# Sliding-window attention and a token mixer: q^T kept in even and odd tokens, the stores cut in four to undo it

## The chip, the cores and the metric

The kernel runs on one core of a Trainium2 chip. The metric is the device time of one execution in microseconds (us); runs of a kernel are compared by their median. One execution is also taken by the hardware profiler; its trace names TensorE (PE, with its weight loads as PEld), VectorE (DVE), ScalarE (ACT), GpSimd (POOL) and SyncE (SP), and the DMA queues that POOL and SP issue to.

## What is computed

Eight batches, eight heads, 576 tokens, head dimension 64. Attention looks back over a window of 128 tokens and subtracts a slope times the distance. Its output, 512 wide, is x for a token mixer: a weight for each pair of tokens from two small projections, the mix over all tokens, a ReLU, and an output projection.

```python
scores = scale * np.matmul(q, k.transpose(0, 1, 3, 2))
bias = slopes[:, None, None] * (-np.abs(rel).astype(np.float32))[None, :, :]
mask = (rel >= 0) & (rel < window)            # window = 128
attn = softmax(np.where(mask, scores + bias[None], -1e9))
x = np.matmul(attn, v)                        # (B, H, S, D) -> (B, S, H * D)
W_tok = scale * np.einsum('bsd,btd->bst', x @ w_q, x @ w_k)
out = np.maximum(np.einsum('bst,btd->bsd', W_tok, x), 0.0) @ w_out
```

The mixer's sum over t runs over all tokens, so the order in which tokens lie there does not matter to it; the rows of `out` come in the order of the rows s.

## The kernel before

All work is a list of 796 small operations, written down batch by batch (`load_qk`, `load_v`, `transposes`, `attention` with `values`, `mixing`). A string of numbers, `ORDER`, then fixes the order in which they are emitted, and so the order on each engine: `57P7` is operation 57 on TensorE with its result in PSUM bank 7, `62A` operation 62 on ScalarE, D is VectorE, G is POOL, S is SyncE; `+13/7` puts 13 matmuls on zeros ahead (`keep`), which fill a wait. Every engine works through its own list in order and waits on semaphores for what an operation needs. Nothing is moved while it runs.

The stages of a batch:

- Loads (L239), all issued by POOL, cast fp32 to f16 on the way. q and k of batches 1 to 5 come in pair form: a partition holds two neighbouring tokens, 128 elements in one run for each head. For batches in `ONE` (6 and 7) a partition holds one token, 64 elements a run, and there are twice as many issues of half the size. The last 64 tokens of q and k come in one tile `ntl`. Batch 0 has six tokens to a partition, in space borrowed from `osa`.
- Transposes (`tqk`, L366 in pair form and L360 in one-token form; `tqkt` L382 for the tail) put q^T and k^T in PSUM, even tokens ahead of odd ones where pairs were loaded. The copy out of PSUM (`etqk`, on ScalarE L220 or VectorE L222) puts them in token order into `qkT`: its source is read with a stride of 128 elements between neighbours.
- `sc` (L415): scores of two heads in eight or ten small matmuls, k^T as weights, a strip of q^T moving. Columns of a strip are queries. `exp` (L420) on ScalarE, `edge` (L435) and `mul` (L439) on VectorE multiply with `bt`, the exponentials of slope times distance, made from `rel` (an iota, L245).
- `pv` (L459) multiplies with v, whose extra column gives the softmax sum; `rec` and `nrm` (L472, L475) normalize into x; `xt` (L491) transposes x, `ext` copies it out.
- `mixing`: `wqk` (L508), `wkt` (L526), `g` (L538), `mx` (L554) with its ReLU `emx`, then `po` (L575): four matmuls for 128 rows of the output of a pair of batches. `eo` copies the bank into one of 14 tiles of `osa`, and `st` (L582) is its store, issued by SyncE. There are 36 of each; a tile is used again for the store 14 later, after the earlier one has landed.

SyncE has nothing but the stores. They stand in its queue in the order of `ORDER`, and at the head stands operation 318, which waits for copy 317 on ScalarE. SyncE's DMAs use eight semaphores in turn, so a store also waits for the one eight issues before it to land.

Of the kernel before, what the change touches and what calls it, by code (L numbers as in the profile page):

```python
# [13 lines left out]
P = 128  # L14
S = 576
# [11 lines left out]
0D 1D 32G 2G 28G 3D 22D 31G 4D 30G 29G 33G 137G 23D 6A 9A 53P7+13/7 35G 7A 11A 45P6 34G 134G 51P5+4/0 136G 52A  # L27
49P4 21G 50D 47P5+3/0 46D 133G 72P0 48A 74P2 55P4 132G 8A 5A 54A 40G 63P5+3/6 75A 59P7 39G 60D 12A 73A 36G 13D
61P2+3/2 16D 76D 43G 57P1+1/7 62A 56D 149P7 17G 64A 38G 147P0 85P2 58A 65D 135G 148D 18A 94P4 86A 150D 145P6
44G 95A 96P2+1/0 146D 83P0 97A 143P5+1/7 37G 10A 77D 42G 144A 14D 41G 78P2+1/4 84A 98D 228G 79D 186P6+3/4 80D  # L30
26G 87D 164P4+2/0 19D 99D 25G 151P3+1/0 165A 142G 66D 100P0 15A 152A 138G 88D 67P4 187A 188P2 139G 101D 68D
102D 189A 89P6 140G 69D 175P0 81P3 176A 141G 90D 166P4 91D 103P2 229G 104A 82D 92P7+2/0 190D 177P0 167A 153P2
232G 191D 178A 70P6+1/6 227G 24D 240P5+2/4 168D 71A 93D 231G 154A 179D 105P6+1/0 180D 321G 20A 241A 155P0 169D
230G 106A 107A 320G 108P5+1/2 170P2 109A 192P6 322G 156A 193D 244P5 194D 324G 110P4 181P0 171D 319G 172D 111A
245A 112P6 416G 182D 157D 114P2 238P4 115A 158D 242P5 323G 113A 118P2 239A 119D 159P6 234G 243D 195P3 160D
183D 270P4 246P2 235G 161D 116P0 247A 117D 173P7 336P6 419G 174D 271A 272P0 337D 184P2 273A 338P7 418G 196A
274D 248P0 250P4 237G 275D 332P6 249A 251A 339D 283P0 233G 162P3 281P4 163A 252D 333D 185A 236G 282A 334P7
197P2 27G 253D 284A 259P4 329G 335A 198D 330P6 260A 414G 285D 200P7 431P1 199A 201D 261P4 325G 331D 432A 202P7
417G 262A 203D 353P0 340P2 286D 415G 210P6 354A 351P4 211D 352A 326G 254P0 263D 341A 276P6 255D 327G 256D
364P4 362P2 264D 363A 287P0 365A 328G 277D 129P3 288D 278D 342P4 511G 289D 130A 375P6 257P2 343A 265P0 510G  # L40
126P3 344D 376A 258D 601G 429P5 345D 290P4 127A 208P6 291A 266D 433P3 507G 267D 209A 425P2 355D 279P4 434A
366D 268P7 509G 373P0 280D 430A 269D 204P3 426D 374A 516G 206P6 427P5 207A 292P0 605G 356D 428A 346P6 508G
205D 293A 123P5 347D 294A 506G 348D 295P4 448P2 377D 296A 705G 435P0 124D 449A 297P7 421G 436A 459P4 298D
357P2 367D 424G 460A 301P0 457P6 302A 358D 368P4 359D 458A 602G 446P0 369D 468P2 447A 370D 521P7 422G 349P6
469A 378D 305P0 470P4 423G 471A 212P3 461D 350D 306A 522D 437P4 420G 472D 299P6 303P0 438A 519P2 304D 213A
523P5 439D 706G 520A 517P4 462D 379P0 610G 518A 300D 120P3 606G 380D 524A 221P2 381D 697G 121D 371P7 222A
616P6 698G 450D 372A 382P5 617D 527P0 383A 609G 360P4 451D 538P2 361A 525P7 604G 440D 528A 384P4 514G 539A
526D 560P0 385A 607G 452P2 386D 387P7 215P6 561A 603G 453D 388A 562P4 454D 608G 216A 529P0 389P7 563A 473D
699G 716P6 530A 441P2 564D 512G 540P4 717D 551P0 390D 620P6 513G 442D 552A 224P7 621D 565D 541A 515G 463P0
225A 443D 391P4 700G 549P6 464D 392D 622P3 550A 702G 444P2 623D 618P5 445A 703G 397P6 465D 393P3 624P2 398A  # L50
619D 704G 395P0 394A 712P7 531D 396A 626P5 701G 625D 637P3 627A 474P0 532D 615G 307P2 638A 475D 713D 639P5
613G 308A 476D 714P4 640A 614G 533P2 715D 650P0 612G 542D 628P6 310P5 534D 629A 553D 543D 611G 466P4 651A
720P7 707G 535D 311A 218P6 709G 721A 630D 648P0 641D 544P2 631D 711G 649A 718P7 545D 219A 708G 566P0 546D 719A
455P5 567D 313P6 710G 467D 456A 568D 733P2 735P4 554D 632P0 736A 316P7 633D 314A 634D 555P4 734A 724P0 317A
556D 722P2 477P6 557D 725A 318S 217S 125S 399P7 131S 128S 220S 478D 723A 744P0 642D 661P4 659P2 745A 411P6
652D 737D 400A 726D 405P1 660A 653D 401S 547P7 662A 727D 643P2 412A 569P0 548D 406A 479P4 413S 226S 644D 570A
645D 536P7 480D 558P6 408P3 559D 481A 482P2 537D 755P0 409D 483A 746P4 757P6 756A 663D 410S 571P2 214S 315S
664D 747A 484P1 758A 572D 665P4 485D 573A 748D 574P7 646P6 666D 575A 488P0 667D 490P2 489A 576P7 486P4 491A
728P0 577D 487A 647D 492P2 582P6 729D 635P5 730D 583A 494P4 493A 759D 578P0 636D 584P6 580P2 760D 579A 497P5
581A 738D 654P0 585A 761P2 495A 655D 656D 739P6 498A 496S 223S 122S 309S 407S 500P4 749D 731P5 740D 668P1 762D  # L60
741D 732A 402P0 669D 750P6 763D 742P5 403A 657P1 751D 752D 586P3 404S 312S 658A 764P2 743A 753P7 765D 670P0
754D 587D 766P6 671D 589P5 672D 767A 673P3 769P2 590D 503P1 674D 592P5 501D 504A 770D 675P3 768A 505S 499S
502S 588S 591S 771P4 676A 593A 677P0 683P2 772D 595P7 678A 594S 684D 775P4 773P0 596D 679P2 598P6 776A 680D
597S 774A 681P4 779P2 599A 777P0 685P7 682D 778A 600S 780D 694P6 686A 784P5 687S 695D 691P4 696S 785D 790P7
786S 692D 793P6 693S 791D 688P5 792S 794D 787P4 795S 689A 781P7 690S 788D 789S 782A 783S
# [86 lines left out]
ONE = (6, 7)  # L152
# [6 lines left out]
def kernel(  # L159
# [20 lines left out]

    bt = pool.tile([P, H, 512], F16, name="bt")
# [5 lines left out]
    vn = [pool.tile([P, NT, H, VW], F16, name=f"vn{i}") for i in range(NV)]  # L187
    qkT = [pool.tile([P, 2, 4, S], F16, name=f"qkT{i}") for i in range(NQ)]
# [52 lines left out]
    def setup():  # L241
# [3 lines left out]
                lambda e: nc.gpsimd.iota(rel, pattern=[[1, 256]], base=0, channel_multiplier=-1),  # L245
                writes=["rel"])
        plan.op("idn", ("DVE",),
                lambda e: nc.vector.tensor_scalar(out=idn, in0=rel[:, 0:128], scalar1=0, scalar2=None,
# [44 lines left out]
    def load_qk(b):  # L293
# [35 lines left out]
    def transposes(b):  # L329
        T = qkT[b % NQ]  # L330
        if b == 0:
            for hp in range(4):
                for x in range(2):
# [8 lines left out]
                    def ev(e, hp=hp, x=x, g=g):  # L342
                        cp(e, T[:, x, hp, :].rearrange("t (p j) -> t p j", j=6),
# [6 lines left out]
        for z in range(2):  # L350
            for x in range(2):
                g = Ps(1)

                def tr(e, z=z, x=x, g=g):
                    o = ps16(g).rearrange("t (y j p) -> t y j p", y=4, j=2)
                    if b in ONE:
# [11 lines left out]
                def ev(e, z=z, x=x, g=g):  # L368
                    if b in ONE:
# [268 lines left out]
```

## Time and profile before

| what | value |
|---|---|
| median of 3 runs | 147.66 us (147.45 to 148.08) |
| the profiled execution: time, and span of the program in it | 148.28 us, 146.2 us |
| busy in the span: PE, DVE, ACT, POOL | 134.8, 122.2, 109.6, 86.1 us |
| first and last store issue | 101.3 and 143.0 us |

Busy time is the time in which an engine worked, and its share is an average over stages. Matmuls are pipelined, so a busy PE is not one at its peak. The chain that ended last is followed back from the last instruction to what released it; the stages are read with tables by windows of time. SPq is SyncE's sequencer issuing a DMA: the time given is the issue, not the transfer.

### The profile page before, as it was taken

The page shows a single profiled execution, that of the slowest core. Times are in us where ns is not written, and L with a number is a line of the kernel's source. Part 1 is how long each engine was busy: PE and PEld are TensorE (multiplying, and loading weights), DVE is VectorE, ACT ScalarE, POOL GpSimd, SP SyncE. Part 2 cuts the span into 40 slices and gives each one's busy share as a digit, 9 for nine tenths or more (in the row PEclk, how much of TensorE's full clock was granted, in tenths as well). Part 3 has the DMA queues.
Part 4 walks back from the last instruction along what each step waited for, and adds up shares of the span by engine and source line. Part 5 has one row for each costly group of instructions (what it writes and reads, how often), then busy time and mean ns, then how long its engine had stood idle before and what let it go on. Part 6 is the DMA issues. An engine that isn't in the chain of part 4 may idle for free.

```text
span 146.2 us, 5403 instructions
## 1 busy us (share of the span) xinstructions
PE 134.8 (92%) x2319; PEld 87.9 (60%) x2319; DVE 122.2 (84%) x229; ACT 109.6 (75%) x172; POOL 86.1 (59%) x114
## 2 busy tenths in 40 slices
PE   6979889999898889999999999999989999999990
PEld 2444547667675566767667676676667577653430
DVE  3634899977999998999999999998989898868750
ACT  3329969897699987999999889899959872557121
POOL 6999999999578976898899999910000000000000
PEclk9999999999999999999999999999999999999997
DMA  2999999999999999999999999990957018329684
GB/s 28 135 171 178 162 142 140 132 162 179 178 173 159 178 178 164 166 169 173 154 153 137 149 152 155 136 128 12 378 193 281 8 59 300 147 97 376 259 321 172
DMA packets 90855, 24.59 MB, mean 168 GB/s; under 512 B 84176, under 2 KB 86224, under 8 KB 90832
## 3 DMA queue, kind: packets, MB, share of 16 engines
q0 software_dynamic: 85648, 14.82, 130.2%
q1 hardware_dynamic: 5184, 9.44, 17.4%
q8 instruction: 18, 0.29, 0.7%
q14 instruction: 5, 0.04, 0.1%
HBM read 29.62 MB, written 9.44 MB: 267 GB/s over the span
## 4 chain that ended last, share of the span: by engine, by line
PE 45%; ACT 20%; DVE 14%; DMA 10%; issue 6%; POOL 2%; SPq 1%; ACTq 0%; DVEq 0%; POOLq 0%
PE psb L575 15%; ACT pt L420 9%; PE psb L459 7%; DMA out_dram<-osa 6%; PE psb L415 5%; DMA osa<-in_k_dram 4%; DVE x L475 4%; PE psb L491 3%; ACT qkT L220 3%; ACT rm L561 3%; PE psb L360 3%; PE psb L366 3%; ACT xT L220 2%; PE psb L554 2%; PE psb L508 2%
## 5 line engine op out<-in xcount | busy, mean ns | idle before, releaser
L420 ACT ACTIVATE pt<-psb 128x768 f16<-128x768 f32 x64 | 49.8, 819 | 6.2 <-PE psb L415 5.2
L239 POOL DMA_DIRECT2D vn<-in_v_dram x44 | 36.6, 887 | 3.6 <-DMA natq<-in_q_dram 2.4
L575 PE MATMUL psb<-wout,rm 128*128 128x512 f16 x144 | 35.2, 379 | 0.2
L439 DVE TENSOR_TENSOR pt<-pt,bt 128x1536 f16<-128x1536 f16 x32 | 29.9, 949 | 0.2
L475 DVE TENSOR_TENSOR x<-psb,inv 128x640 f16<-128x640 f32 x32 | 26.0, 820 | 0.7
L459 PE MATMUL psb<-vn,pt 128*128 128x65 f16 x576 | 22.4, 193 | 1.6 <-DVE pt L439 0.5
L222 DVE COPY qkT<-psb 128x1024 f16<-128x1024 f16 (+2 forms) x23 | 18.7, 822 | 5.6 <-PE psb L339 5.1
L459 PEld LDWEIGHTS <-pt 128*128 128x128 f16 x576 | 20.1, 97 | 5.0 <-issue 1.2
L220 ACT COPY osa<-psb 128x512 f32<-128x512 f32 x23 | 13.3, 590 | 12.3 <-PE psb L575 6.9
L220 ACT COPY qkT<-psb 128x1024 f16<-128x1024 f16 (+2 forms) x20 | 17.8, 912 | 4.2 <-PE psb L339 2.9
L415 PE MATMUL psb<-qkT 64*64 64x192 f16 (+2 forms) x640 | 20.1, 234 | 0.9 <-ACT qkT L220 0.4
L575 PEld LDWEIGHTS <-rm 128*128 128x128 f16 x144 | 12.7, 98 | 12.7 <-issue 1.1
L415 PEld LDWEIGHTS <-qkT 64*64 64x64 f16 x640 | 11.6, 106 | 9.7 <-issue 7.0
L239 POOL DMA_DIRECT2D natk<-in_k_dram x18 | 16.2, 938 | 1.7 <-DMA natk<-in_k_dram 1.2
L239 POOL DMA_DIRECT2D natq<-in_q_dram x18 | 16.8, 938 | 0.0
L592 PE MATMUL psb<-wz 128*128 128x512 f16 x43 | 13.8, 427 | 1.5 <-DVE wz L242 1.3
L491 PE MATMUL psb<-idn,x 128*128 128x128 f16 x160 | 13.6, 219 | 0.9 <-ACT osa L220 0.5
L435 DVE TENSOR_TENSOR pt<-pt,bt 128x512 f16<-128x512 f16 x32 | 12.9, 414 | 1.2 <-ACT pt L420 1.0
L561 ACT ACTIVATE rm<-psb 128x576 f16<-128x576 f32 x21 | 12.8, 653 | 1.5 <-PE psb L554 1.0
L491 PEld LDWEIGHTS <-x 128*128 128x128 f16 x160 | 10.0, 98 | 3.9 <-issue 1.1
L222 DVE COPY osa<-psb 128x512 f32<-128x512 f32 x13 | 9.0, 689 | 2.7 <-PE psb L575 2.3
L220 ACT COPY xT<-psb 128x576 f16<-128x576 f16 x15 | 9.4, 647 | 1.8 <-PE psb L491 1.8
(62 smaller groups left out, 162.2 us busy)
## 6 DMA issues: line engine op xcount, KB each, us to landing
out_dram<-osa SPq DMA_DIRECT2D x36, 256.0 KB, 2.9
vn<-in_v_dram POOLq DMA_DIRECT2D x28, 128.0 KB, 4.9
natq<-in_q_dram POOLq DMA_DIRECT2D x10, 256.0 KB, 6.8
natk<-in_k_dram POOLq DMA_DIRECT2D x10, 256.0 KB, 7.2
vn<-in_v_dram POOLq DMA_DIRECT2D x16, 64.0 KB, 4.8
natq<-in_q_dram POOLq DMA_DIRECT2D x8, 128.0 KB, 5.2
natk<-in_k_dram POOLq DMA_DIRECT2D x8, 128.0 KB, 5.1
osa<-in_q_dram POOLq DMA_DIRECT2D x4, 144.0 KB, 4.1
```

The lines of the kernel that those rows point to most:

```text
L220: nc.scalar.copy(o, i)
L222: nc.vector.tensor_copy(out=o, in_=i)
L239: plan.op(name, ("POOL",), lambda e: nc.gpsimd.dma_start(out=dst, in_=src), reads=reads, writes=writes)
L415: nc.tensor.matmul(ps32(g)[half : half + 64, o : o + w], T[r, 1, hp, k0 : k0 + 64], T[r, 0, hp, q0 : q0 + w], start=True, stop=True)
L420: nc.scalar.activation(out=blocks(pt)[:, :, 2 * u : 2 * u + 2, 0:192], in_=ps32(g).rearrange("t (a c) -> t a c", a=2)[:, :, 0:384].rearran ...
L439: nc.vector.tensor_tensor(out=o, in0=o, in1=bt[:, 2 * hp : 2 * hp + 2, 0:192].unsqueeze(2).broadcast_to([P, 2, 4, 192]), op=ALU.mult)
L459: nc.tensor.matmul(ps32(g)[:, o : o + D + 1], pt[:, a, c : c + 128], vv[:, kb, 2 * hp + a, 0 : D + 1], **flags)
L475: nc.vector.tensor_tensor(out=xb[:, :, 128 * hp : 128 * hp + 128].rearrange("t j (a d) -> t a j d", a=2), in0=px()[:, :, :, 0:D], in1=iv.u ...
L491: nc.tensor.transpose(ps16(g)[:, 128 * t : 128 * t + 128], xb[:, t, 128 * hp : 128 * hp + 128], idn)
L561: nc.scalar.activation(out=o, in_=s, func=AF.Relu, scale=WSCALE)
L575: nc.tensor.matmul(ps32(g), rm[p % NR][:, db, o : o + 128], wout[:, db, :], start=(db == 0), stop=(db == 3))
L592: nc.tensor.matmul(psb[:, b, :], wz[:, 0:P], wz[:, 0:DM], start=True, stop=True)
```

## The change

q^T is no longer put in token order when it leaves PSUM. It is kept as all even tokens and then all odd ones, so the copy reads its source densely. The score matmul takes its strip from there in pieces of 32: for each 64 tokens, 32 even ones and then 32 odd ones. From there on, every strip, the table `bt` (through `rel`), x, and the rows of the output have this order inside each block of 64 tokens. k^T and v stay in token order. The identity `idn` is put together again from the permuted `rel`.

The output has to be in token order. A store of 128 rows holds two blocks of 64, each of 32 even and 32 odd tokens, and becomes four DMAs of 32 rows, each to every second row of `out`.

q is loaded in pair form for all batches from 1 on, and k in pair form for 1 to 3 and one-token form for 4 to 7 (`ONE`). The tail copy becomes two copies, one for q and one for k. `ORDER` is new throughout: 36 matmuls on zeros instead of 43, other places for loads, and other engines for some copies. Of the 28 copies `etqk`, VectorE had 8 strided and 6 dense ones and has 1 and 13; ScalarE had 12 and 2 and has 5 and 9. ScalarE takes over three `eo`, two `emx` and three `ewqk` on balance.

On SyncE, the stores around the 17th (`osa` is the tile, `out_dram` the output; DMAHW are the eight slots of SyncE's own queue, DMASW those of POOL's, the others the engine that copied the bank). Before, the 15th to the 19th:

```order
L582 DMA out_dram<-osa 128x512 [waits DMAHW6_49]
L582 DMA out_dram<-osa 128x512 [waits DMAHW7_49,DMASW0_49]
L582 DMA out_dram<-osa 128x512 [waits DMAHW0_49]
L582 DMA out_dram<-osa 128x512 [waits DMAHW1_49,Activation_49]
L582 DMA out_dram<-osa 128x512 [waits DMAHW2_49,DMASW0_49]
```

After, the 16th (from its second piece on), the 17th and the head of the 18th:

```order
L603 DMA out_dram<-osa 32x512 [waits DMAHW5_49]
L603 DMA out_dram<-osa 32x512 [waits DMAHW6_49]
L603 DMA out_dram<-osa 32x512 [waits DMAHW7_49]
L603 DMA out_dram<-osa 32x512 [waits DMAHW0_49,Activation_49]
L603 DMA out_dram<-osa 32x512 [waits DMAHW1_49]
L603 DMA out_dram<-osa 32x512 [waits DMAHW2_49]
L603 DMA out_dram<-osa 32x512 [waits DMAHW3_49]
L603 DMA out_dram<-osa 32x512 [waits DMAHW4_49,Activation_49]
```

What was one row is four, each with a slot of its own; only the first piece waits for the bank. In the new table the 17th store is 595 and its bank is copied by 594A; behind 594A stand 14 `po`, 8 `mx`, one `g` and one `wkt` on TensorE. Behind 317A, which the first store waits for in both, stand 7 `sc`, 7 `pv`, 13 `xt`, 23 `po`, 4 `wqk`, 4 `wkt`, 4 `g` and 16 `mx` before, and one `sc`, two `pv` and one `xt` more after.

On VectorE, around the copies of batch 0 (`qkT_82`) and batch 1 (`qkT_83`). Before:

```order
L222 COPY qkT_82<-psb 128x576
L435 TENSOR_TENSOR pt_86<-pt_86,bt 128x2x4x64
L222 COPY qkT_83<-psb 128x8x64
L222 COPY qkT_83<-psb 128x4x256 x2
L439 TENSOR_TENSOR pt_87<-pt_87,bt 128x2x4x192
L268 COPY bt<-bt 128x4x64 x2
```

After:

```order
L224 COPY qkT_83<-psb 128x8x128
L272 COPY bt<-bt 128x4x64 x2
L452 TENSOR_TENSOR pt_87<-pt_87,bt 128x2x4x64
L456 TENSOR_TENSOR pt_87<-pt_87,bt 128x2x4x192
L230 MEMSET pt_88 128x2x64
L224 COPY qkT_83<-psb 128x8x32
L224 COPY qkT_83<-psb 128x4x64
L452 TENSOR_TENSOR pt_88<-pt_88,bt 128x2x4x64
L224 COPY qkT_83<-psb 128x8x128
```

The two strided copies of a batch (128x4x256) have become two dense ones of q (128x8x128), with those of k on ScalarE here, and the tail (128x8x64) has become two rows.

On POOL, the k of batch 4 (`natk_74`). Before:

```order
L239 DMA vn_79<-in_v_dram 128x8x64
L239 DMA natq_71<-in_q_dram 128x8x128
L239 DMA vn_79<-in_v_dram 64x8x64
L239 DMA natk_74<-in_k_dram 128x8x128 x2
L239 DMA vn_79<-in_v_dram 128x8x64 x3
```

After:

```order
L241 DMA natk_74<-in_k_dram 128x8x64
L241 DMA ntl_77<-in_q_dram 64x8x64
L241 DMA natk_74<-in_k_dram 128x8x64
L241 DMA wout<-in_moe_w_out_dram 128x4x512
L241 DMA ntl_77<-in_k_dram 64x8x64
L241 DMA natq_71<-in_q_dram 128x8x128
L241 DMA vn_79<-in_v_dram 128x8x64 x2
L241 DMA vn_79<-in_v_dram 64x8x64
L241 DMA vn_79<-in_v_dram 128x8x64 x2
L241 DMA natk_74<-in_k_dram 128x8x64 x2
```

Two issues have become four of half the size, and they start ahead of the second half of the batch's q (`natq_71`) and end behind the v of batch 3 (`vn_79`).

```diff
 ORDER = """
-0D 1D 32G 2G 28G 3D 22D 31G 4D 30G 29G 33G 137G 23D 6A 9A 53P7+13/7 35G 7A 11A 45P6 34G 134G 51P5+4/0 136G 52A
+0D 1D 30G 35G 21A 2G 31G 3D 4D 33G 29G 28G 32G 8A 12A 136G 6A 59P7+13/7 34G 49P6+1/0 37G 50D 51P5+2/0 134G 60D
...
-ONE = (6, 7)
+ONE = (4, 5, 6, 7)
...
         plan.op("iota", ("POOL",),
-                lambda e: nc.gpsimd.iota(rel, pattern=[[1, 256]], base=0, channel_multiplier=-1),
+                lambda e: nc.gpsimd.iota(rel, pattern=[[64, 4], [1, 2], [2, 32]], base=0, channel_multiplier=-1),
                 writes=["rel"])
...
-                if b in ONE:
+                if x == 1 and b in ONE:
                     for j in range(2):
...
                     def ev(e, hp=hp, x=x, g=g):
+                        if x == 0:
+                            cp(e, T[:, x, hp, :].rearrange("t (j p i) -> t j p i", j=2, i=3),
+                               ps16(g)[:, 0:S].rearrange("t (i j p) -> t j p i", i=3, j=2))
+                            return
                         cp(e, T[:, x, hp, :].rearrange("t (p j) -> t p j", j=6),
                            ps16(g)[:, 0:S].rearrange("t (j p) -> t p j", j=6))
...
                 def ev(e, z=z, x=x, g=g):
+                    if x == 0:
+                        cp(e, T[:, x].rearrange("t y (j p) -> t y j p", j=2)[:, :, :, P * z : P * z + P],
+                           ps16(g).rearrange("t (y j p) -> t y j p", y=4, j=2))
+                        return
                     if b in ONE:
...
-                    cp(e, T[:, :, :, 512:576], ps16(g)[:, 0:512].rearrange("t (y x c) -> t x y c", y=4, x=2))
+                    s = ps16(g)[:, 0:512].rearrange("t (y x c) -> t x y c", y=4, x=2)
+                    cp(e, T[:, 0].rearrange("t y (j p) -> t y j p", j=2)[:, :, :, 256:288],
+                       s[:, 0].rearrange("t y (p j) -> t y j p", j=2))
+                    cp(e, T[:, 1, :, 512:576], s[:, 1])
...
-                            nc.tensor.matmul(ps32(g)[half : half + 64, o : o + w],
-                                             T[r, 1, hp, k0 : k0 + 64], T[r, 0, hp, q0 : q0 + w],
+                            n = w // 64
+                            d = ps32(g)[half : half + 64, o : o + w].rearrange("t (s j m) -> t s j m", s=n, j=2)
+                            s = T[r, 0, hp, :].rearrange("t (j s m) -> t s j m", j=2, m=32)
+                            nc.tensor.matmul(d, T[r, 1, hp, k0 : k0 + 64], s[:, q0 // 64 : q0 // 64 + n],
                                              start=True, stop=True)
...
             def st(e, o=o, n=n):
-                nc.sync.dma_start(out=out[2 * p : 2 * p + 2].rearrange("b t c -> (b t) c")[o : o + 128, :], in_=osb[n])
+                d = out[2 * p : 2 * p + 2].rearrange("b t c -> (b t) c")
+                for z in range(2):
+                    for j in range(2):
+                        r = 64 * z + 32 * j
+                        nc.sync.dma_start(out=d[o + 64 * z : o + 64 * z + 64, :].rearrange("(m j) c -> m j c", j=2)[:, j],
+                                          in_=osb[n][r : r + 32])
```

More of the change, by code (lines that the diff above doesn't have):

```diff
@@ L32 @@
[L32 to L61, printed above, removed]
@@ L66 @@
+507S 413S 680D 684A 777P0 685P6 599P3 778A 686D 682A 496P1 500D 600D 501S 602P0 497D 773P2 498S 775P4 601S
+779P6 407S 696P1 774A 780D 776A 687P3 603A 697A 787P2 604S 688D 693P7 689S 698S 788D 781P6 789S 694A 784P5
+695S 782A 690P4 783S 785D 793P7 786S 691A 790P6 692S 794D 795S 791A 792S
 """
@@ L355, in tr @@
                     o = ps16(g).rearrange("t (y j p) -> t y j p", y=4, j=2)
-                    if b in ONE:
+                    if x == 1 and b in ONE:
                         w = nat[x][n][:, z].rearrange("p (j e) -> p j e", j=2)
```

47 lines of the change are left out of this document (38 added, 9 removed).

## The prediction

> **What bounds the kernel now.** I read the page's share of engines first, then the engines by stage, then the chain that ended last, and then SyncE's queue, because the change quadruples what that queue issues.
>
> ```profile
> PE 134.8 (92%) x2319; PEld 87.9 (60%) x2319; DVE 122.2 (84%) x229; ACT 109.6 (75%) x172; POOL 86.1 (59%) x114
> ...
> DMA  2999999999999999999999999990957018329684
> ```
> ```profile
> 10.00:54.00 44.00, 39.77 (x875) 27.83 (x876) 38.11 (x70) 37.72 (x59) 39.70 (x51) 1.00 1.92 163
> 54.00:98.00 44.00, 43.60 (x831) 30.41 (x828) 41.73 (x79) 40.49 (x62) 37.69 (x45) 1.00 2.23 155
> 98.00:125.00 27.00, 26.23 (x433) 17.95 (x432) 24.79 (x48) 20.08 (x34) 0.00 (x0) 1.00 0.46 169
> 125.00:146.20 21.20, 17.18 (x117) 8.39 (x115) 12.46 (x20) 8.09 (x15) 0.00 (x0) 0.96 0.64 236
> ```
>
> The columns of the second fence are stretch, length, busy PE, PEld, DVE, ACT, POOL, granted clock, DMA share, GB/s. TensorE is never far from full: 39.8 of 44 us, 43.6 of 44, 26.2 of 27. Loads fill the DMA engines until about 98 us (nines), and only then do the stores begin. The end of the chain is TensorE work alone:
>
> ```profile
> 134.44 7.89 PE psb L575 x36
> 142.34 0.02 issue
> 142.36 0.58 ACT osa L220
> ```
>
> The last matmul ends at 142.36 us, ScalarE copies the last bank, and SyncE sends it. So before the change, TensorE sets the end, and SyncE only follows. How closely it follows:
>
> ```profile
> L582 SPq DMA_DIRECT2D out_dram<-osa x36: 332/382/1548, 101.3 to 143.0; - x36
> L582 SPq EVENT_SEMAPHORE  x23: 17/17/28, 10.8 to 142.6; - x23
> ...
> DMA to landing us min/median/max: 2.0/2.9/4.8
> ```
> ```profile
> 119.18 0.33 SPq L582 DMA_DIRECT2D out_dram<-osa  x1
> ```
> ```profile
> 119.57 0.43 SPq L582 DMA_DIRECT2D out_dram<-osa  x1
> ```
> ```profile
> 120.05 1.55 SPq L582 DMA_DIRECT2D out_dram<-osa  x1
> ```
> ```profile
> 142.97 0.33 SPq L582 DMA_DIRECT2D out_dram<-osa  x1
> ```
> ```profile
> SPq L582 <- ACT osa L220: 108.5, 9, 90.5
> ```
>
> The reader is to see four things. One issue occupies SyncE for at least 0.332 us, and a free one starts the next 0.39 us later (119.18 to 119.57). A second one close behind it takes 0.43 us, and its successor starts 0.48 us later (119.57 to 120.05). SyncE does nothing until 101.33 us: its queue is in order, and the store at its head waits 90.5 us for its bank. And the last issue starts at 142.97, lands 2.0 us later, and the span closes 1.2 us after that, at 146.2.
>
> **The change, term by term.**
>
> *Stores.* 36 issues of 128 rows become 144 of 32. The bytes are the same, but SyncE's time is not. Its price for 32 rows is in no row, so I bound it. At the low end it goes with the rows: 0.39/4 = 0.10 us. At the high end it is the spacing inside a burst, 0.48 us. The nearest rows on how an issue depends on its number of runs are POOL's:
>
> ```profile
> L239 POOL DMA_DIRECT2D natq<-in_q_dram x18 | 16.8, 938 | 0.0
> ...
> L239 POOL DMA_DIRECT2D osa<-in_q_dram x4 | 2.8, 698 | 0.9 <-POOLq L622 0.9
> ```
>
> 192 runs cost 698 ns there and 1024 runs 938 ns, 0.3 ns a run: nearly all of an issue is fixed. [...] I take 0.39 − 96 × 0.0003 = 0.36 us, and keep 0.10 and 0.48 as ends. The first piece of a store waits for two semaphores (bank and slot), one more 17 ns instruction with its gap: about 0.05 us. A store thus costs 4 × 0.36 + 0.05 = 1.49 us of SyncE, and 36 cost 53.6 us.
>
> What time is there for it? The same store (entry 318, waiting for copy 317A) heads the queue in both. Behind that copy the new table has one `sc`, two `pv` and one `xt` more than the old. Prices of TensorE groups, from the chain:
>
> ```profile
> 90.83 0.29 PE psb L415 x8
> ...
> 93.64 0.28 PE psb L491 x5
> ```
> ```profile
> 79.25 0.65 PE psb L459 x18
> 79.90 0.15 PE psb L526 x5
> 80.05 0.86 PE psb L575 x4
> ...
> 81.37 0.67 PE psb L538 x10
> ```
> ```profile
> 88.07 0.23 PE psb L554 x2
> ```
>
> That is 0.29 + 2 × 0.65 + 0.28 = 1.9 us. Before, 142.36 − 101.33 = 41.0 us of TensorE stood behind it; now about 42.9. SyncE needs 53.6, so it can no longer follow. The place that decides is further back. The 17th store in the queue waits for copy 594A. Behind that copy TensorE has 14 `po` (0.86), 8 `mx` (0.23), one `g` (0.67) and one `wkt` (0.15) left: 12.04 + 1.84 + 0.67 + 0.15 = 14.7 us. SyncE reaches this store early (16 stores, 23.8 us after the first) and waits; then it has 20 stores, 29.8 us, against 14.7 us of TensorE.
>
> A slot is reused after eight issues, 2.9 us at this pace, longer than the 2.0 us landing, so semaphores add nothing. Copies that reuse a bank of `osa` wait for old stores: 694A needs the 26th store landed (10 stores after the 17th: 127.3 + 14.9 + 2.0 = 144.2 by the sum below), and will wait some 6 us. Three copies behind it on ScalarE wait too, and the last two `po` wait for their PSUM banks, so TensorE's last matmul slips to about 146.5. SyncE is still further behind, so this costs nothing more. In exchange one stall of before goes, since the first reuses come later after the first store:
>
> ```profile
> ACT osa L220 <- DMA out_dram<-osa: 2.5, 1, 2.5
> ```
>
> *q^T copies.* On VectorE a 128x1024 copy with a strided source takes 1218 ns and a dense one 676; on ScalarE, 1032 (strided) and 1038 (dense), no difference:
>
> ```profile
> L222 DVE COPY qkT<-psb 128x1024 f16<-128x1024 f16 x6 | 7.2, 1218 | 0.1
> ```
> ```profile
> L222 DVE COPY qkT<-psb 128x1024 f16<-128x1024 f16 x5 | 3.4, 676 | 0.1
> ```
> ```profile
> L220 ACT COPY qkT<-psb 128x1024 f16<-128x1024 f16 x12 | 12.1, 1032 | 1.3 <-PE psb L366 1.3
> ```
> ```profile
> L220 ACT COPY qkT<-psb 128x1024 f16<-128x1024 f16 x2 | 2.1, 1038 | 0.0
> ```
>
> The old table has 8 strided and 6 dense ones on VectorE, the new 1 and 13: 7 × 0.54 = 3.8 us off VectorE, most of it beside a fuller TensorE. The tail copy splits in two, 7 more instructions:
>
> ```profile
> L222 DVE COPY xT<-psb 128x576 f16<-128x576 f16 x17 | 7.4, 448 | 1.1 <-PE psb L491 0.9
> ...
> L222 DVE COPY qkT<-psb 128x512 f16<-128x512 f16 x5 | 2.1, 419 | 0.2 <-PE psb L382 0.2
> ```
>
> Each half lies between 0.21 and 0.42 us, so a split adds 0 to 0.42; I take 0.3, six on VectorE, 1.8 us back. The new table also hands work to ScalarE:
>
> ```profile
> L222 DVE COPY osa<-psb 128x512 f32<-128x512 f32 x13 | 9.0, 689 | 2.7 <-PE psb L575 2.3 <-ACT wT L220 0.3
> L563 DVE TENSOR_SCALAR rm<-psb 128x576 f16<-128x576 f32 x11 | 8.1, 748 | 0.9 <-PE psb L554 0.7 <-ACT rm L561 0.2
> ...
> L222 DVE CAST wT<-psb 128x576 f16<-128x576 f32 x4 | 3.0, 754 | 0.5 <-PE psb L508 0.5
> ```
>
> Three of the first, two of the second and three of the third leave VectorE, 5.8 us, and some 1.3 us of small copies come to it. In all VectorE loses 3.8 − 1.8 + 4.5 = 6.5 us; ScalarE, with more idle time, takes about 5.
>
> *Score matmuls* read q in runs of 32. The tail copy of the old kernel reads runs of 64 at no cost (512 in 419 ns, 576 dense in 448), while runs of one cost 1218/676 = 1.8. At that far end 64 groups of 0.29 us would grow by 15 us; I take zero, being nearest to 64. *Transposes:* q of batches 6 and 7 and k of 4 and 5 swap forms, 4 tiles each way, zero. *Loads:* both tables issue 36 for q and k.
>
> ```profile
> natk<-in_k_dram POOLq DMA_DIRECT2D x10, 256.0 KB, 7.2
> ...
> natk<-in_k_dram POOLq DMA_DIRECT2D x8, 128.0 KB, 5.1
> ```
>
> With eight in flight these land every 0.9 and 0.64 us; a chunk in one-token rows costs 1.28 instead of 0.9. Four such chunks come 1.5 us later by batch 5, and batches 6 and 7 give it back; TensorE waited for no load after 10 us, so 0 to 1.5 us. *Keep-warm matmuls* go from 43 to 36, some 0.22 us each where TensorE waited anyway: 0 to 1.5 us gained.
>
> Together (VectorE's relief, the stall, the loads) I let TensorE end 1.0 us earlier if no store holds it, at 141.4, with −3.5 to +1.5 around it.
>
> **The sum.** 141.4 − 14.7 + 0.59 (copy) = 127.3, when store 17 may go. Plus 29.8: SyncE is done at 157.1, its last issue starts at 156.8. Plus 2.0 landing and 1.2 closing: span 160.0. The profiled execution took 148.28 for a span of 146.2, so 162.1 by it; the median of the runs, 147.66, lies 0.6 below it: 161.5 us.
>
> [...]
>
> **The rivals.**
> 1. *The issue goes with the rows* (not slower). At 0.10 us, 20 stores cost 9 us against 14.7, and SyncE follows again. The end is 141.4 + 0.6 + three more pieces 0.3 + 2.0 + 1.2 = 145.5, or 147.0 us as a median; 145.8 if TensorE ends a further 1.2 us earlier. It decides below 0.17 us an issue, where 20 × (4 × 0.17 + 0.05) = 14.6 us. [...] Against: a free issue is 332 ns exactly, and POOL's slope. [...] Chance 0.15.
> 2. *Between the two*, 0.17 to 0.30 us, half fixed: at 0.25, 20 × 1.05 = 21 us, 152.7 us. Chance 0.13.
> 3. *Bursts stay at 0.48 us:* what makes a second issue wait is fixed for each DMA. 20 × 1.97 = 39.4, 171 us. Against: the longer second issue is plainest where much is in flight, and a piece has a quarter of it. Chance 0.10.
>
> The forecast has 0.62; within it 0.30 to 0.42 us an issue moves the time from 156.7 to 166.3, the end of TensorE by up to 2.5 more. For 8 in 10 the range takes in the middle case down to 149 and part of the third up to 170. Faster by over 0.5% (about what a measurement of this kernel can tell) needs rival 1 with TensorE's gain: 0.08. Within it: 0.05. Slower: 0.87.
>
> **What would show it.** SyncE's issues after: x144, a minimum near 0.33, unbroken from the 17th store to the end. The chain ends on SyncE and DMA, not on L592; TensorE's last matmul stands some 13 us before the end; ScalarE waits on a store once, for some 6 us, near the end. VectorE's busy time falls to about 116 us. A minimum below 0.17 us, or TensorE in the last 3 us of the chain, proves me wrong.

## The result, and the profile after

The changed kernel takes 177.33 us (175.86 to 177.76), the kernel before, run on the same chip, 147.87 us (147.45 to 148.53): a ratio of 1.197, with a 95% interval of 1.188 to 1.206. Slower was forecast, but 161.5 us, and 177.3 lies outside the range of 149 to 170. The profiled execution took 177.0 us for a span of 175.2, 29 us more than before.

The page of the kernel after, shares of the engines, DMA engines in 40 slices, and the chain that ended last:

```profile
PE 138.0 (79%) x2312; PEld 88.8 (51%) x2312; DVE 116.6 (67%) x228; ACT 113.2 (65%) x180; POOL 86.3 (49%) x114
...
DMA  3999999999999999999999945455453545555553
...
PE 30%; SPq 14%; DMA 14%; POOL 13%; ACT 8%; DVE 6%; issue 5%; ACTq 0%; POOLq 0%; DVEq 0%
```

No engine works much more than before (TensorE 138.0 against 134.8 us, VectorE 5.6 less, ScalarE 3.6 more). TensorE's 3.2 us go with a lower granted clock, 0.93 over the span against 0.99 before: the same matmuls of 128x512 took 399 ns in the mean, before 379. What is new is SyncE's queue in the chain, with 14%, and DMA engines that are half full to the end, where before they had idle and full slices. The same kernel by stages (columns as in the prediction: stretch, length, busy PE, PEld, DVE, ACT, POOL, granted clock, DMA share, GB/s; the last stretches are cut elsewhere than before):

```profile
10.00:54.00 44.00, 38.36 (x859) 27.11 (x850) 38.20 (x81) 36.13 (x54) 39.06 (x52) 1.00 1.89 159
54.00:98.00 44.00, 43.40 (x840) 30.32 (x837) 41.48 (x80) 41.20 (x63) 38.43 (x46) 1.00 2.23 157
98.00:125.00 27.00, 23.91 (x411) 17.24 (x409) 21.57 (x42) 18.59 (x33) 0.00 (x0) 0.94 0.52 120
125.00:150.00 25.00, 20.23 (x132) 9.39 (x130) 8.31 (x15) 10.15 (x18) 0.00 (x0) 0.93 0.48 122
150.00:175.20 25.20, 3.33 (x8) 0.99 (x7) 2.07 (x3) 2.15 (x4) 0.00 (x0) 0.61 0.52 133
```

From 10 to 98 us the two kernels are alike, within 1.6 us for each engine and stretch. Everything is lost behind the first store: TensorE has 8 matmuls left after 150 us, and the DMA engines move 120 to 133 GB/s where before they moved 169 and 236. SyncE's queue after, by its line, and by its timeline (start, length, and how many issues were put together):

```profile
L603 SPq DMA_DIRECT2D out_dram<-osa x144: 314/424/1582, 99.1 to 172.6; - x144
...
  ACT osa L222: 18.3, 3
  DVE osa L224: 6.0, 2
...
DMA to landing us min/median/max: 1.6/1.7/3.7
```
```profile
99.08 73.95 SPq L603 DMA_DIRECT2D out_dram<-osa  x144
```
```profile
131.65 0.42 SPq L603 DMA_DIRECT2D out_dram<-osa  x1
```
```profile
134.08 0.31 SPq L603 DMA_DIRECT2D out_dram<-osa  x1
```

From 99.08 us on, the 144 issues take 73.95 us. The row alone does not show that they follow each other, for this view puts the issues of a queue together even where the queue stood between them. Issue by issue they do: each starts 0.04 to 0.12 us after the end of the one before, too soon for a wait for a slot, with two exceptions. The 17th store starts 2.0 us after the 16th (131.65 + 0.42 to 134.08, the last two fences), the 18th 0.5 us after the 17th. Last, the chain near its end:

```profile
146.80 0.37 SPq L603
147.21 0.42 SPq L603
147.68 0.43 SPq L603
148.15 0.43 SPq L603
148.68 0.37 SPq L603
...
153.80 1.72 DMA out_dram<-osa
155.62 0.59 ACT osa L222
156.26 3.34 PE psb L592 x8
159.62 0.59 ACT osa L222
```

One group of four is 0.41 + 0.47 + 0.47 + 0.53 = 1.88 us (146.80 to 148.68), the median of all groups too. Who waits for whom has turned round: a store lands (153.80), then ScalarE may copy into its tile of `osa` (155.62), and then TensorE's last eight matmuls have a bank (156.26). TensorE ends at 159.6 us, 13.4 us ahead of SyncE.

### The profile page after: what moved, and what is told of

Same layout as the page of the kernel before. It is cut to its first block, busy times and chain, and to the rows that moved or that the text cites. A ratio compares the mean times of both kernels' runs of the same rounds, so it can differ in the third digit from the quotient of the medians.

```text
span 175.2 us, 5516 instructions
## 1 busy us (share of the span) xinstructions
PE 138.0 (79%) x2312; PEld 88.8 (51%) x2312; DVE 116.6 (67%) x228; ACT 113.2 (65%) x180; POOL 86.3 (49%) x114
## 4 chain that ended last, share of the span: by engine, by line
PE 30%; SPq 14%; DMA 14%; POOL 13%; ACT 8%; DVE 6%; issue 5%; ACTq 0%; POOLq 0%; DVEq 0%
SPq L603 14%; PE psb L592 9%; DMA natq<-in_q_dram 9%; POOL vn L241 6%; PE psb L476 5%; POOL osa L241 3%; DMA out_dram<-osa 3%; PE psb L571 3%; PE psb L508 3%; ACT pt L437 3%; PE psb L433 2%; DMA vn<-in_v_dram 2%; ACT osa L222 2%; PE psb L555 2%; PE psb L374 2%
## 5 line engine op out<-in xcount | busy, mean ns | idle before, releaser
L592 PE MATMUL psb<-wout,rm 128*128 128x512 f16 x144 | 37.8, 399 | 7.5 <-ACT osa L222 7.5
L222 ACT COPY osa<-psb 128x512 f32<-128x512 f32 x26 | 15.2, 599 | 23.6 <-DMA out_dram<-osa 18.3
L241 POOL DMA_DIRECT2D natk<-in_k_dram x22 | 20.7, 957 | 3.5 <-DMA natq<-in_q_dram 1.7
L224 DVE COPY qkT<-psb 128x1024 f16<-128x1024 f16 (+2 forms) x31 | 17.4, 584 | 4.8 <-PE psb L343 4.2
L222 ACT COPY qkT<-psb 128x1024 f16<-128x1024 f16 (+2 forms) x19 | 16.7, 902 | 4.2 <-PE psb L374 2.5
L578 ACT ACTIVATE rm<-psb 128x576 f16<-128x576 f32 x23 | 14.5, 654 | 7.1 <-PE psb L571 6.9
L224 DVE COPY osa<-psb 128x512 f32<-128x512 f32 x10 | 6.7, 686 | 12.7 <-PE psb L592 6.7
L241 POOL DMA_DIRECT2D natq<-in_q_dram x14 | 13.2, 956 | 0.9 <-PE psb L571 0.9
L614 PE MATMUL psb<-wz 128*128 128x512 f16 x36 | 12.5, 454 | 1.3 <-DVE wz L244 1.3
L571 PE MATMUL psb<-wT,gm 64*128 64x288 f16 x32 | 8.2, 316 | 3.3 <-ACT osa L222 3.0
```

The lines of the kernel that those rows point to most:

```text
L222: nc.scalar.copy(o, i)
L224: nc.vector.tensor_copy(out=o, in_=i)
L241: plan.op(name, ("POOL",), lambda e: nc.gpsimd.dma_start(out=dst, in_=src), reads=reads, writes=writes)
L578: nc.scalar.activation(out=o, in_=s, func=AF.Relu, scale=WSCALE)
L592: nc.tensor.matmul(ps32(g), rm[p % NR][:, db, o : o + 128], wout[:, db, :], start=(db == 0), stop=(db == 3))
```

## The experiments

All times are medians; ratios are to the kernel before, run beside each. "Leaves order out" marks kernels whose output rows stay in even and odd tokens inside a block of 64.

| run | what | us | ratio (95%) |
|---|---|---|---|
| e1 | changed, one store of 128 rows (leaves order out) | 146.73 | 0.993 (0.989 to 0.997) |
| e2 | before, four stores of 32 rows | 178.68 | 1.210 (1.203 to 1.216) |
| e3 | changed, two stores of 64 rows (leaves order out) | 157.25 | 1.063 (1.053 to 1.072) |
| e4 | changed, one store, order put right by the mixer's reads | 150.61 | 1.020 (1.013 to 1.028) |
| e5 | the same by its writes | 149.68 | 1.012 (1.009 to 1.016) |
| e6 | before, stores cut in six ways | 170.79 | one execution |
| e7 | changed, stores not held back | 170.84 | 1.151 (1.143 to 1.158) |
| e8 | changed, two stores of 64 rows in three dimensions | 294.71 | 1.994 (1.986 to 2.002) |
| e9 | changed, two stores of 256 columns (leaves order out) | 151.18 | 1.020 (1.013 to 1.026) |
| e10 | changed, stores on SyncE and ScalarE | 176.43 | 1.189 (1.183 to 1.194) |
| e11 | changed, stores on SyncE and GpSimd | 155.32 | 1.050 (1.046 to 1.054) |
| e12 | changed, stores on three queues | 163.87 | 1.106 (1.100 to 1.112) |

### e1 and e2: the stores alone, from both sides

e1 takes the four stores out of the changed kernel, e2 puts them alone into the kernel before, as 32 neighbouring rows each.

```diff
-                d = out[2 * p : 2 * p + 2].rearrange("b t c -> (b t) c")
-                for z in range(2):
-                    for j in range(2):
-                        ...
+                nc.sync.dma_start(out=out[2 * p : 2 * p + 2].rearrange("b t c -> (b t) c")[o : o + 128, :], in_=osb[n])
```

> The changed kernel with each output tile sent by one DMA of 128 rows again. It leaves out putting the rows of a block of 64 tokens back in order, so only its time is meant. Theory A, the price of an issue on SyncE is fixed for each DMA (about 0.47 us in a burst): with 36 issues TensorE sets the end again, the first store near 99 us, median 145 to 148 us. Theory B, the time went elsewhere (scores that read q in runs of 32, the new order, loads of k): it stays above 165 us, with TensorE as busy after 98 us as in the changed kernel.

```diff
-                nc.sync.dma_start(out=out[2 * p : 2 * p + 2].rearrange("b t c -> (b t) c")[o : o + 128, :], in_=osb[n])
+                d = out[2 * p : 2 * p + 2].rearrange("b t c -> (b t) c")
+                for r in range(0, 128, 32):
+                    nc.sync.dma_start(out=d[o + r : o + r + 32, :], in_=osb[n][r : r + 32])
```

> The kernel before, with each output tile sent in four DMAs of 32 neighbouring rows. Nothing else differs and the output stays in order. Theory A: 144 issues at 0.47 us from 101.3 us are 68 us and more, so the last one near 170 to 173 us, median 174 to 179 us. Theory B: within 3 us of before, 148 to 151 us. Theory C, it is the writing of every second row that is slow, not the issue: these pieces have no gaps, so 148 to 155 us, with issues spaced below 0.3 us.

Measured: 146.73 and 178.68 us. The four stores alone cost the kernel before 31.1 us, and without them the rest of the change gains 0.7%. SyncE's timeline of e2, and its line in e1:

```profile
100.96 73.67 SPq L584 DMA_DIRECT2D out_dram<-osa  x144
```
```profile
L599 SPq DMA_DIRECT2D out_dram<-osa x36: 332/393/1363, 98.3 to 141.2; - x36
```

144 issues of neighbouring rows take 73.67 us, those of every second row 73.95, with gaps of 1.9 and 2.5 us in all within. So neither the new order of the work nor the spread of the rows in memory is the cause; the number of DMAs, or their size, is.

### e3, e6 and e9: number or size?

> The changed kernel with two DMAs of 64 neighbouring rows for each tile; the rows inside a block of 64 stay out of order, so only its time is meant. Theory A: spacing in a burst again 0.47 us at 64 rows; 72 issues; behind the 17th store 20 stores need 20 x 0.94 + 1 = 20 us against 14.7 us of TensorE, so about 5 us over one store for each tile: 150 to 154 us. If the price goes with the rows above a fixed half, spacing near 0.35 us at 64 rows and a time within 1.5 us of one store for each tile.

Measured: 157.25 us, over the 150 to 154 expected. An issue of 64 rows took 0.47 us at least and 0.595 in the median, dearer than 32 rows and dearer than 128:

```profile
L602 SPq DMA_DIRECT2D out_dram<-osa x72: 466/595/1683, 100.5 to 152.5; - x72
```

That contradicts a fixed price for each DMA, so e6 prices shapes next to each other.

```diff
+SIZES = ((128,), (64, 64), (32,) * 4, (16,) * 8, (96, 32), None)
+                cut = SIZES[(9 * p + o // 128) % 6]
+                if cut is None:
+                    ...
+                r = 0
+                for y in cut:
+                    nc.sync.dma_start(out=d[r : r + y, :], in_=osb[n][r : r + y])
+                    r += y
```

(`None` is two halves of 256 columns with all 128 rows; the lines for it are left out here.)

> The kernel before, whose 36 stores of 128 rows are cut in six ways, in turn: one of 128 rows; two of 64; four of 32; eight of 16; 96 and 32; two halves of 256 columns with all 128 rows. Every output row is stored as before. It prices a store's issue on SyncE by its shape. Seen so far: 128 rows 0.33 us, 64 rows 0.47 to 0.60 us, 32 rows 0.31 to 0.42 us. If the price has a fixed part and a part by row, 16 rows take less than 32 (0.25 to 0.30 us) and 96 more than 64 (0.6 to 0.8 us), with 128 an exception. If it is one price of 0.31 to 0.33 us and the 64-row pieces an exception, 16 rows take 0.31 us and 96 rows 0.33 us. The halves of 256 columns: 0.33 us if rows or DMAs set the price, less if bytes do. The time of the whole, by some 108 stores between the one of 72 (157.3 us) and that of 144 (178.7 us): 160 to 172 us.

Measured: 170.79 us, inside the 160 to 172 expected; the prices expected, 0.25 to 0.33 us for 16 rows and 0.33 or 0.6 to 0.8 for 96, were those of free issues or went by the row, and neither came. SyncE's timeline of e6, looked at in short windows that hold one kind each: 16 rows (two groups of eight), 32 rows (one group), two halves of 256 columns, 96 and 32 rows, and two of 64 rows:

```profile
127.14 7.33 SPq L591 DMA_DIRECT2D out_dram<-osa  x16
```
```profile
155.38 1.77 SPq L591 DMA_DIRECT2D out_dram<-osa  x4
```
```profile
157.25 0.87 SPq L587 DMA_DIRECT2D out_dram<-osa  x2
```
```profile
158.22 0.87 SPq L591 DMA_DIRECT2D out_dram<-osa  x2
```
```profile
164.84 1.11 SPq L591 DMA_DIRECT2D out_dram<-osa  x2
```

The lengths divided by the count give 0.46 us for 16 rows, 0.44 for 32 and for the other two, and 0.56 for 64. Median issues were 0.418 us for 16 rows, 0.425 for 32, 0.395 for 128 (mostly first in a group; the second of a burst took 0.43 before) and 0.432 for 256 columns. Half the rows do not make an issue cheaper, nor do half the bytes: a DMA in a burst costs SyncE some 0.42 us and the next starts 0.05 later. 64 rows are an exception of 0.14 to 0.17 us for which no run here has a reason.

e9 tests that as a whole kernel: 72 DMAs again, but not of 64 rows.

```diff
+                d = out[2 * p : 2 * p + 2].rearrange("b t c -> (b t) c")[o : o + 128, :]
+                for c in range(0, DM, 256):
+                    nc.sync.dma_start(out=d[:, c : c + 256], in_=osb[n][:, c : c + 256])
```

> The changed kernel with two stores for each 128 rows, each of all 128 rows and 256 of the 512 columns (as with the one store, the rows of a 64-token block are left in even and odd tokens, which leaves the output's order out and nothing of the work). 72 issues, as with the two stores of 64 rows that took 157.3 us. If a DMA costs SyncE 0.42 us and the next starts 0.47 later whatever its rows, and pieces of 64 rows (0.60) are an exception, a group costs 0.94 us, the last 17 or 18 groups about 17 us against TensorE's 15, and the time is 149 to 151.5 us. If two DMAs cost as much as those of 64 rows because the bytes or the number of groups decide it, 157 us.

Measured: 151.18 us, inside the 149 to 151.5 expected for a price by the DMA, and 6 us under e3. Its 72 issues took 0.444 us in the median, and TensorE ended at 141.4 us, SyncE at 147.7. In these runs the number of DMAs sets the price, at 0.42 to 0.44 us each, and the shape adds to it for 64 rows (0.595 us).

### e7: the late start

The changed kernel holds all stores back until copy 317A. e7 puts each group behind its copy in the list.

```diff
-... 317A 661P2 549D 663P4 550D 662A 318S 559P6 128S 315S 214S 125S 664A 131S
+128S 427P7 508G ... 130A 131S ... 124A 125S ... 317A 318S
```

> The changed kernel with its 144 stores, but each group of four is issued as soon as its copy stands in the list of instructions, not held back behind the copy 317A; nothing else is moved. If SyncE's dispatch of 1.9 us for each group of four is the bound, the early start (about 17 groups are out before the late ones are ready) takes the first 32 us off the queue, yet the last 16 to 18 groups still come within some 15 us and need 1.9 us each: about 32 us against 15, an end some 10 to 18 us later than TensorE's, 156 to 166 us. If only the late start of the stores costs the time, the end falls to 146 to 150 us.

Measured: 170.84 us, 6.5 us better than the change, and a miss: above the 156 to 166 expected. Stretches of e7, the last one shorter:

```profile
54.00:98.00 44.00, 39.43 (x746) 27.17 (x742) 37.84 (x72) 37.73 (x57) 36.47 (x44) 1.00 2.11 188
98.00:125.00 27.00, 25.09 (x433) 18.05 (x433) 22.22 (x41) 20.81 (x37) 1.92 (x3) 0.94 0.74 109
125.00:150.00 25.00, 23.89 (x206) 12.66 (x202) 13.10 (x25) 14.05 (x25) 0.00 (x0) 1.00 0.44 113
150.00:169.00 19.00, 0.00 (x0) 0.00 (x0) 0.63 (x2) 0.00 (x0) 0.00 (x0) 0.58 0.50 129
```

Two things happen. The early stores run beside the loads, in a stretch where the DMA engines are full (share 2.11; 2.23 in the change): they take up to 6.5 us to land instead of 1.7 in the median, the last load lands at 107.3 us instead of 100.1, and TensorE loses 4.0 us of work between 54 and 98 (39.43 against 43.40). And from the 20th group on SyncE has no gap again: 17 groups take 32.9 us and end at 166.8, while TensorE ends at 148.9. SyncE's issues of that tail, in one row:

```profile
133.84 32.94 SPq L603 DMA_DIRECT2D out_dram<-osa  x68
```

The tail bound stays; the estimate had left out what the early stores take from the loads.

### e4 and e5: the order put right on TensorE

Both let each 128 rows leave by one DMA in token order, since the mixer puts the order right. e4 reads wT and wq2 in token order: neighbouring columns come in turn from two places 32 elements apart, and it writes PSUM densely. e5 reads them densely and writes every second element of a PSUM bank. Strips are 320 and 256 columns, so that they hold whole blocks of 64.

```diff
-                                          (wq2 if a else wT)[m][r, 288 * c : 288 * c + 288], start=True, stop=True)
+                        x = (wq2 if a else wT)[m][r, f : f + w].rearrange("t (s j m) -> t s m j", j=2, m=32)
+                        d = ps32(g)[:, 512 * a : 512 * a + w].rearrange("t (s m j) -> t s m j", j=2, m=32)
```

(e4; e5 has `t s j m` on the right of both.)

> The changed kernel with tokens put back in order by TensorE: the mixing matmuls read the weights of the mixer as moving operand in token order (two elements 32 apart, then on by one), in strips of 320 and 256 instead of 288 and 288; one DMA of 128 rows for each tile; the output is in order. Theory A with a moving operand whose stride costs nothing: as one store for each tile, 145 to 148 us. If single elements with a stride cost as they do VectorE (1.8 times), 64 matmuls of 0.12 us of stream grow by about 6 us in all, most of it on the path: 150 to 154 us.

> The changed kernel with q^T, the transposes and the scores as they are, but the token order is put right again where the mixing matmuls write PSUM: they read their moving operand densely, in even and odd tokens, and write every second element of a bank, in strips of 320 and 256 columns; so each 128 rows leave in token order by one store (36 stores in place of 144). If TensorE's cost lay in reading the moving operand with a stride (469 ns for 320 columns where 288 dense ones took 317 ns), a strided write is another thing and may cost nothing: the matmuls of 320 columns take 340 to 360 ns, TensorE is busy about 134 us, and the kernel takes 146 to 147.5 us, as with one unordered store. If a strided write of PSUM costs what the strided read did, they take about 470 ns and the time is about 150.6 us. If the dispatch of the stores is not the cause of the loss at all, the time stays over 160 us.

Measured: 150.61 and 149.68 us. The mixing matmuls by shape, before, in e4 and in e5:

```profile
L554 PE MATMUL psb<-wq,gm 64*128 64x288 f16 x32 | 7.5, 289 | 0.0
```
```profile
L573 PE MATMUL psb<-wq,gm 64*128 64x320 f16 x16 | 6.9, 469 | 0.0
```
```profile
L573 PE MATMUL psb<-wq,gm 64*128 64x320 f16 x16 | 6.4, 450 | 0.0
```

288 dense columns took 289 ns, so 320 would be about 321 (estimated by columns). By the recorded lengths the reads in turn cost some 148 ns a matmul and the writes of every second element 129: hardly a difference, so the hope for free writes in e5's expectation fell. Both kernels are slower than the one before, but by 2.0 and 1.2% and not by 20.

### e8: fewer DMAs by an address pattern

```diff
                 for z in range(2):
-                    for j in range(2):
-                        ...
+                    r = 64 * z
+                    nc.sync.dma_start(out=d[o + r : o + r + 64, :].rearrange("(m j) c -> j m c", j=2), in_=osb[n][r : r + 64])
```

> The changed kernel with the same rows stored to the same places, but two DMAs for each 128 rows in place of four: one for each block of 64 rows, whose destination is an address pattern of three dimensions (even or odd, 32 rows, 512 columns). 72 issues in place of 144. If the issue's price goes by rows and not by the pattern, it is that of the two contiguous stores of 64 rows (0.60 us each, 0.64 apart): about 157 us. If a pattern of three dimensions costs more to work out, 0.8 us or more each and 163 us or more. If the number of DMAs alone set the price (0.47 us each): about 151 to 153 us.

Measured: 294.71 us, far beyond the 163 us from which the dearest expectation starts. The shortest issue took 0.51 us, the median one 2.44. SyncE's line in e8, and the stretch of 130 to 180 us:

```profile
L602 SPq DMA_DIRECT2D out_dram<-osa x72: 511/2442/4500, 99.3 to 277.6; - x72
```

```profile
130.00:180.00 50.00, 18.34 (x204) 11.47 (x204) 10.27 (x20) 10.14 (x18) 0.00 (x0) 0.67 0.13 51
```

The DMA share is 0.13 and the rate 51 GB/s; 128 KB at 51 GB/s are 2.6 us, near the 2.44 of the median issue. So by these figures the issue goes at the pace of the transfer here: the two stores of 64 rows in e3, with the same bytes and no pattern of even and odd rows, took 0.595 us an issue. 0.13 is as much as two of the 16 DMA engines would give that are always busy (estimated: 2/16 = 0.125); how the transfer is spread over them, and what in the pattern slows it, was not shown.

### e10, e11 and e12: a second dispatcher

The same 144 DMAs of 32 rows, handed to more queues.

```diff
-                        nc.sync.dma_start(out=...
+                        q = (nc.sync, nc.scalar)[j]        # e10
+                        q = (nc.sync, nc.gpsimd)[j]        # e11
+                        q = (nc.sync, (nc.scalar, nc.gpsimd)[z])[j]   # e12
+                        q.dma_start(out=...
```

> The changed kernel whose two stores of even tokens of each group go out on SyncE's queue and whose two of odd tokens on ScalarE's. The rows, pieces and places are the same. If SyncE's dispatch is the bound, SyncE has 72 issues (34 us) and no longer ends last; ScalarE gets 72 of some 0.42 us, 30 us of dispatch in a stretch in which it was busy 29 of 50 us, so it becomes late itself: 150 to 158 us. If it were not the dispatch but the transfers or their landing that bound the tail, the time stays at 170 us or more.

> The same with GpSimd's queue for the two stores of odd tokens. GpSimd has nothing to do after its last load at about 107 us, but a DMA issue there took 0.85 us (loads of 128 KB): 72 of them would be 61 us. If the price on GpSimd goes by the DMA too, it ends at 165 us or later and bounds the kernel in SyncE's place, 163 to 172 us; if it goes by rows (32 in place of 64 to 128), 0.3 to 0.5 us and the kernel ends with TensorE, 147 to 151 us.

> The same with the four stores of a group on three queues: two on SyncE, one on ScalarE, one on GpSimd. SyncE 72 issues (34 us), ScalarE 36 (15 us), GpSimd 36 (at 0.85 us, 31 us). No queue should need more than the 49 us that TensorE's work behind the first store takes: if the dispatch alone cost the time, 147 to 151 us, within 2% of the kernel with one unordered store. If the number of DMAs costs something else (transfers, landing, waits), it stays over 155 us.

Measured: 176.43, 155.32 and 163.87 us. e11 is the clearest, by its line on both queues:

```profile
L604 SPq DMA_DIRECT2D out_dram<-osa x72: 314/420/1878, 98.3 to 145.0; - x72
L604 POOL DMA_DIRECT2D out_dram<-osa x72: 498/498/542, 98.6 to 145.5; - x72
```

With the same number of DMAs, the same pieces and the same places, the last issue is at 145.5 us instead of 172.6, and TensorE ends at 141.2, as in e1 (140.5). SyncE's own issues kept their price beside the second queue (0.420 us in the median). So the dispatch on one queue was the bound, and neither the transfers nor their landing. An issue on GpSimd took 0.498 us, not the 0.85 of its loads, and its last load was issued by 95.3 us, not 107. The time is still 155.3, between the 147 to 151 and the 163 to 172 us that were expected, because GpSimd is held at the end by an instruction that the trace names DRAIN:

```profile
L656 POOLq DRAIN x3: 46/102/7563, 145.0 to 153.1; - x3
```

The longest of the three ran from 145.0 to 152.6 us, while SyncE's last issue ended at 145.4. The kernel before has a DRAIN of GpSimd at 93.5 to 99.0 us, before its first store at 101.3 and 47 us ahead of the end.

e10 is a miss: 150 to 158 expected, almost nothing gained. ScalarE's waits in e10 (in a profiled execution of 178.5 us, 2 over the median), and its timeline around the first of them:

```profile
ACT osa L222 <- DMA out_dram<-osa: 11.3, 4, 3.8
ACT rm L578 <- DMA out_dram<-osa: 10.4, 2, 6.2
ACT pt L437 <- DMA out_dram<-osa: 9.0, 2, 4.8
```
```profile
101.14 4.96 ACTq L604 DMA_DIRECT2D out_dram<-osa  x9
106.16 0.81 ACT L437 ACTIVATE pt<-psb 128x768 f16<-128x768 f32 x1 [4.78 <-DMA out_dram<-osa]
```

The expectation counted 30 us of dispatch on ScalarE, but not that the issues stand in line with the exponentials and copies, four to nine at a time. The view puts the waits down to older stores that land, but most of them is ScalarE issuing: in the 30.7 us of the three rows it issued 51 stores, which took 21.8 us; only the rest is gaps and waits between them. TensorE fell to 17.5 us of work between 98 and 125 (26.2 before) and ended at 169.5. e12 has half of that on ScalarE (`pt` waits 6.1 us in two) and lies in between, outside the 147 to 151 expected.

## Why the prediction was right or wrong

- **What bounds it after: right.** SyncE's queue of 144 issues sets the end, the chain ends on SPq and landings, and TensorE is done 13.4 us earlier than SyncE. e2 and e11 show the cause from both sides.
- **The price of an issue: the term that failed.** I took 0.36 us, the free issue of 128 rows less a slope taken from GpSimd. The runs show two errors. A free price was used for a queue that is never free: the free issue is 0.314 us, but in a burst it is 0.42 with the next 0.05 later, and 36 groups make nothing but a burst. And there is no slope by rows to take off: 16 and 32 rows (0.418 and 0.425 us) cost what the second of two issues of 128 rows cost before (0.43). The group was priced at 1.49 us and measures 1.885. The row with the burst's spacing, 0.48, stood in the profile of before; I dismissed it for the main case because I laid it to bytes in flight. The trace of before spoke against that: the second issues at 101.73, 110.52, 119.57 and 130.16 us all took 0.43 us, after the busy stretch of the loads as well as after pauses of 1.3 to 7.7 us. And e6's pieces of 16 rows, with an eighth of the bytes, show 0.46. What SyncE does in these 0.42 us no run shows.
- **"SyncE reaches this store early and waits": wrong, and from the same term.** At 1.885 us the first 16 groups are 30.2 us, and long issues (below) add 2.8: SyncE came to the 17th store at 132.1 us, where I had it go at 127.3. Then it waited 2.0 us for copy 594A, which itself waited for a store to land. The miss adds up: the 17th store went 6.8 us late (134.1), the last 20 groups cost 20 × 0.395 = 7.9 us more, another long issue and the gap ahead of the 18th store 1.2 net. That is 15.9 us, and SyncE was done at 173.0 instead of 157.1; the medians differ by 15.8.
- **Rival 3** had the price (171 us at 1.97 a group) but not the late 17th store, and I gave it 0.10. Rivals 1 and 2 are refuted by e2 (0.424 us an issue) and e6.
- **Copies waiting on stores: mechanism right, size not.** I had one wait of 6 us, costing nothing more. There were 18.3 us in 3 on ScalarE and 6.0 in 2 on VectorE:

```profile
ACT osa L222 <- DMA out_dram<-osa: 18.3, 3, 11.1
...
PE psb L592 <- ACT osa L222: 7.5, 1, 7.5
...
DVE osa L224 <- DMA out_dram<-osa: 6.0, 2, 4.8
```

  TensorE's last matmul therefore ended at 159.6 us, not at 146.5. That it costs little more holds: apart from the 2.0 and 0.5 us gaps, SyncE never stood.
- **TensorE's end with no store in the way, 141.4: right.** 140.5 in e1 and 141.2 in e11. The 2.5 us stall on a store is gone in e1, as forecast, and its 0.7% is the gain of about 1 us that was summed.
- **q^T copies: right.** VectorE's busy time fell by 5.6 us (6.5 forecast) and ScalarE's rose by 3.6 (5). The rows of the dense copy and of a half of the tail, after:

```profile
L224 DVE COPY qkT<-psb 128x1024 f16<-128x1024 f16 x14 | 10.0, 723 | 0.4 <-PE psb L368 0.2
...
L224 DVE COPY qkT<-psb 128x256 f16<-128x256 f16 x12 | 3.7, 350 | 0.2 <-PE psb L394 0.2
```

  Two halves of 350 ns against one of 419 to 448 are 0.25 to 0.28 us more a split, where 0.3 was taken.
- **Score matmuls in runs of 32 cost nothing: right.** After and before:

```profile
L433 PE MATMUL psb<-qkT 64*64 64x192 f16 x384 | 19.2, 250 | 0.0
```
```profile
L415 PE MATMUL psb<-qkT 64*64 64x192 f16 x384 | 19.4, 250 | 0.0
```

  384 records of 250 ns lie in 19.2 and 19.4 us of busy time, so by the trace they overlap, alike in both.

- **Landing, 2.0 us: near.** A piece of 32 rows lands in 1.7 us in the median.

## What to carry to other kernels

Price a queue that will be full by the spacing inside a burst (here 0.47 us, 1.885/4), not by a free issue (0.314), and count DMAs before bytes: here four DMAs of 32 rows took SyncE 1.885 us in a burst, one of 128 rows 0.43, or 0.48 to the next. When a stage's stores come from one in-order queue, set their number times that spacing against the time left behind the first of them; where it was more here (36 × 1.885 = 67.9 us against an estimated 42.9), the queue set the end, and a second queue helped only on an engine whose other work could stand in line behind an issue (155.32 us with GpSimd's, 176.43 with ScalarE's). An order that costs something to undo is best undone where that adds no instructions: here 1 to 2% on TensorE, 20% in the stores, and neither is paid for by the 0.7% that the order gained.

## What the runs showed of the hardware that was not expected

- A store of 64 rows of 2 KB costs SyncE more (0.54 to 0.60 us in a burst, at least 0.47 free) than one of 16, 32 or 128 rows (about 0.42; at least 0.31 free for 32 and 0.33 for 128). No run tells why.
- A few issues take 1.2 to 1.9 us. After, the four longest (at 102.33, 109.53, 122.60 and 139.47 us) start within 0.1 us of a packet of 16 KB on the queue that the profile names "instruction" (102.38, 109.46, 122.53, 139.40), and the stores around them land in 2.5 to 3.7 us in place of 1.7. Before, the two issues of 1.27 and 1.55 us (104.94 and 120.05) stand beside two such packets as well (104.90 and 120.28). That they are the cause is an inference; nothing was run to remove them.
- Matmuls of 320 columns are recorded 46% longer when the moving operand comes in turn from two places 32 elements apart (469 ns), and 40% longer when they write every second element of PSUM (450), against an estimated 321 ns for dense ones, while runs of 32 cost nothing.
- GpSimd's longest DRAIN took 5.6 us before, 6.4 after and 7.6 in e11, where it starts shortly before its last DMA issue by the record (145.0 and 145.5 us); before, its 5.6 us lay beside TensorE's work.
